# Rearranging the first two attentions of an attention and mixture-of-experts kernel

## The chip, the cores and the metric

The kernel runs on one core of one Trainium2 chip. The metric is the device time of one execution in microseconds (us). Before the change it is 366.93 us, the median of three runs (366.91 to 367.05). Engine names in the profile: PE is TensorE (matmuls; PEld its weight loads), DVE is VectorE, ACT is ScalarE, POOL is GpSimd, SP is SyncE. [...] everything that matmuls leave in PSUM is copied out by ScalarE or VectorE.

## The reference

Two stages follow each other. The first is grouped-query attention: 8 batches, 16 query heads, 4 key/value heads, 384 positions, head size 64, all float32. The second is a two-level gated mixture of experts over the 3072 tokens (8 x 384) with a model width of 1024: each token picks one of 4 groups by a softmax gate, then one of 4 experts in the group, and gets relu(x w1) w2 of that expert times both gate weights.

```python
scores = scale * np.matmul(q, k.transpose(0, 1, 3, 2))
attn = np.exp(scores - max); attn /= sum
out  = np.matmul(attn, v)                      # x: (3072, 1024)
...
g_idx = argmax(x @ w_group); e_idx = argmax(x @ w_expert[g_idx])
out[t] = g_w * e_w * (relu(x[t] @ w1[g, e]) @ w2[g, e])
```

## The kernel before

The program is written out by hand in order; each engine takes its instructions from a queue of its own, in the order in which the Python code emits them. Nothing is reordered later, so the place of a call in the code is its place in the queue of the engine that it uses.

**Attention.** For each batch there are 24 units: 4 groups of heads (g) times 6 chunks of 64 key positions (c). A unit u = 6g + c is: scores on PE (line 310, four matmuls into a PSUM tile of tag s, of which there are two), the exponential on ScalarE (line 316) into one of 13 buffers e, and the product with v on PE (line 329, eight matmul records, into a PSUM tile of tag o, one tile for each group, two in turn). `Attn.run` emits for each u: the scores of unit u + 2, the product of unit u, then `tail(u)`, and then the calls that a dictionary lists for u. The tail adds e tiles pairwise on GpSimd (line 336, at c = 1 and 3), reduces them on VectorE (line 343, four reductions for each group at c = 3, 4 and 5), and at the end of a group copies the PSUM result to xT, on VectorE (line 379) or on ScalarE (line 381).

**Normalising.** `collect` sums the reductions of some groups on VectorE (line 405), `sums` spreads them over partitions by matmuls (line 415) into a PSUM tile and takes the reciprocal on VectorE (line 419), `spread` transposes it into a tile rb (line 426), and `scale_x` multiplies xT by it (line 435). `cast` makes a bfloat16 copy xb. In `sums`, which "x" means the o tile that the current group does not use; the next group takes that tile over.

**Choosing an expert.** The kernel guesses for each batch one expert whose weights it fetches, from a mean of v: `sum_v` sums v over positions, on VectorE by one reduction (line 461) or on GpSimd by three adds (lines 467 to 469, the first of 768 elements a partition, the others of 256), `guess_mean` (474) and `guess_logits` (489) are small matmuls, `first_choice` (for batch 0) or `gate_softmax` (for the others, with the gate of the batch before it, lines 496 to 521) and `pick_index` (lines 576 to 586; line 580 is a comparison, 583 sums an index) run on VectorE. `pick` reads the index into a GpSimd register (line 590). `pick_w1` and `pick_w2` issue the fetches of 2 MB each (lines 560 and 566) from GpSimd's queue.

**Experts.** `moe_h` does two of the eight column blocks of w1: 16 matmuls (line 622) and a relu on ScalarE (line 626); `moe_y` does w2 (line 633) and scales the output (lines 658 and 660). `gate_logits` is the gate matmul (line 451).

**The first two batches.** Batch 0 has its scores, its products and its normalising in one run of 24 units. In batch 1 the reductions of the first groups are held back on a list (`hold`) and emitted at `a.release`. After unit 15 of batch 1 the run stops; the expert matmuls of batch 0 (`moe_h`, four times) stand in between, with the gate of batch 0 and the guess for batch 1; then units 16 to 23 follow, and `first_block` with `moe_y` of batch 0, the collect and the sums of the last two groups of batch 1, and the start of batch 2. Every later batch has a block of the same kind, which the change leaves as it is.

Of the kernel before, what the change touches and what calls it, by code (L numbers as in the profile page):

```python
# [9 lines left out]
F32 = mybir.dt.float32  # L10
BF16 = mybir.dt.bfloat16
# [7 lines left out]
def kernel(  # L19
# [11 lines left out]
    nc = tc.nc  # L31
    P = 128
    B, Hq, S, D = q.shape
    _, Hkv, _, _ = k.shape
# [5 lines left out]
    KQ = DM // P  # L40
    KG = KQ // Hkv
# [4 lines left out]
    NC = S // H2  # L46
# [14 lines left out]
    gpool = ctx.enter_context(tc.tile_pool(name="gate", bufs=1))  # L61
# [7 lines left out]
    def ps_tile(which, shape=None, dtype=F32):  # L69
        if which == "x":  # L70
            which = f"o{1 - turn['o']}"
        else:
            turn[which] = 1 - turn[which]
            which += str(turn[which])
        return psum.tile(shape or [P, 2, 512], dtype, name="ps_" + which)
# [4 lines left out]
    k16, qraw, vraw, qT, kT = {}, {}, {}, {}, {}  # L80
# [162 lines left out]
    def evac(eng, out_, in_):  # L243
        if eng is nc.scalar:
            eng.copy(out=out_, in_=in_)  # L245
        else:
            eng.tensor_copy(out=out_, in_=in_)
# [44 lines left out]
    xT, xb, reds = {}, {}, {}  # L292

    class Attn:
# [62 lines left out]
        def tail(self, u):  # L357
            b = self.b
            g, c = u // NC, u % NC
            z = u - c  # L360
            if c in (1, 3) and (b, u) != (1, 3):
                self.add(nc.gpsimd, u - 1)
            if (b, g) == (2, 0):
                for n in ((), (1,), (2, 0))[max(c, 3) - 3]:
                    self.reduce(g, n, (z, z + 4, z + 5)[n])
            elif c >= 3:
                self.reduce(g, c - 3, (z, z + 4, z + 5)[c - 3])
            if c == NC - 1:
                self.reduce(g, NR - 1, z + 2)
                if b not in xT:  # L370
                    if b == 1:
                        w = wpool.tile([P, KQ, F], BF16, name="w1")
                        xT[b] = w.rearrange("p a f -> p (a f)").bitcast(F32)[
                            :, :KQ * S].rearrange("p (a n) -> p a n", n=S)
                    else:
                        xT[b] = xpool.tile([P, KQ, S], F32, name="xT", bufs=1)
                dst, src = xT[b][:, KG * g:KG * (g + 1), :], self.oT[g][:, :, :S]
                if b > 1 and g < Hkv - 1 or (b, g) == (1, 1):
                    nc.vector.tensor_copy(out=dst, in_=src)  # L379
                else:  # L380
                    nc.scalar.copy(out=dst, in_=src)  # L381
# [40 lines left out]
    def spread(b, m, which=None):  # L422

        rb = gpool.tile([P, 2, S], F32, name="rb", bufs=2) if which is None else ps_tile(which)[:, :, :S]
        for r in range(2):
            nc.vector.transpose(  # L426
                out=rb[:, r].rearrange("p (j x) -> p j x", x=32),
                in_=inv[b][:, 2 * m + r].unsqueeze(2).to_broadcast([P, NB, 32]))
        return rb

    def scale_x(b, m, rb, eng):
        if b not in xb:
            xb[b] = xpool.tile([P, KQ, S], BF16, name="xb")
        x = xT[b][:, 2 * m:2 * m + 2, :]
        eng.tensor_mul(out=x, in0=x, in1=rb)  # L435

    def normalise(b, m, which=None):
        scale_x(b, m, spread(b, m, which), nc.vector)

    def cast(b, m, eng=None):  # L440
        ks = slice(2 * m, 2 * m + 2)
        evac(eng or nc.scalar, xb[b][:, ks, :], xT[b][:, ks, :])
# [3 lines left out]
    def gate_logits(b, pt):  # L446

        for kq in range(KQ):
            x = xT[b][:, kq, :].rearrange("p (c t i) -> p t c i", t=4, i=32)
            for t in range(4):  # L450
                nc.tensor.matmul(out=pt[32 * t:32 * t + 32, 0, :32 * SC], lhsT=wg[:, kq, :],  # L451
                                 rhs=x[:, t], start=(kq == 0), stop=(kq == KQ - 1))

    vsum = {}

    def sum_v(b, eng):

        vsum[b] = gpool.tile([P, Hkv, D], BF16, name="vsum")
        with nc.allow_low_precision("only serves a guess"):
            if eng is nc.vector:  # L460
                eng.tensor_reduce(out=vsum[b], in_=vraw[b].rearrange("p g (c d) -> p g d c", d=D),  # L461
                                  axis=AX.X, op=ALU.add)
                return
            n = NC // 2 * D
            t = gpool.tile([P, 2, S], F32, name="rb", bufs=2).rearrange(
                "p a s -> p (a s)").rearrange("p (g n) -> p g n", g=Hkv)
            eng.tensor_add(out=t, in0=vraw[b][:, :, :n], in1=vraw[b][:, :, n:])
            eng.tensor_add(out=t[:, :, :D], in0=t[:, :, :D], in1=t[:, :, D:2 * D])
            eng.tensor_add(out=vsum[b], in0=t[:, :, :D], in1=t[:, :, 2 * D:])

    def guess_mean(b, pt):

        for j in range(Hkv // 2):
            nc.tensor.matmul(out=pt[:, 1, j:j + 1],
                             lhsT=vsum[b][:, 2 * j:2 * j + 2, :].rearrange("p g d -> p (g d)"),
                             rhs=onesb[:, :1], start=True, stop=True)
# [6 lines left out]
    def guess_row(pt):  # L483
        return pt[:, 1, 64:64 + NW]

    def guess_logits(vm, pt):
        n = Hkv // 2
        for j in range(n):
            nc.tensor.matmul(out=guess_row(pt), lhsT=vm[:, j:j + 1].to_broadcast([P, P]),
                             rhs=wgd[:, j, :], start=(j == 0), stop=(j == n - 1))  # L490
# [78 lines left out]
    ers, w1s, w2s = {}, {}, {}  # L569
# [19 lines left out]
    def pick(b):  # L589
        ers[b] = nc.gpsimd.value_load(e_is[b][0:1, 0:1], min_val=0, max_val=NE - 1)  # L590
# [24 lines left out]
            j = 2 * c + h  # L615
            yield slice(h * H2, (h + 1) * H2), 2 * (j % SC) + j // SC

    def ffn_h(x, w1, hT, f0, which, mid=None):
        h = ps_tile(which)
        for jj in range(2):  # L620
            for kq in range(KQ):
                nc.tensor.matmul(out=h[:, jj, :S], lhsT=w1[:, kq, (f0 + jj) * P:(f0 + jj + 1) * P],  # L622
                                 rhs=x[:, kq, :], start=(kq == 0), stop=(kq == KQ - 1))
            if mid is not None and jj == 0:
                mid()
        nc.scalar.activation(hT[:, f0:f0 + 2, :], h[:, :, :S], ACT.Relu)  # L626

    def ffn_y(w2, hT, c, which, nhs=(0, 1), y=None, fs=None):
# [17 lines left out]

    hTs = {}

    def moe_h(b, f0, which, mid=None):
        if f0 == 0:  # L650
            hTs[b] = xpool.tile([P, FQ, S], BF16, name="hT", bufs=1)
        ffn_h(xb[b], w1s[b], hTs[b], f0, which, mid)

    def y_out(b, c, y, eng=None):
        ot = opool.tile([P, DM], F32, name="ot")
# [11 lines left out]
    def do(f, *a):  # L667
        return lambda: f(*a)
# [30 lines left out]
        pick_index(0)  # L699

    def first_fetch():
        pick(0)
        transposed(1)
        pick_w1(0)

# [20 lines left out]
    def second_scale():  # L726
# [3 lines left out]
    a = at[0]  # L730
    a.run(0, NU, {
        1: [do(first_q, GB, GB, "x", nc.vector)],
        3: [cast_k],
        4: [gate_matrix_b, do(sum_v, 0, nc.gpsimd)],
        6: [do(collect, 0, 0, 1)],
        7: [do(first_q, 2 * GB, 2 * GB, "x", nc.vector)],
        8: [do(first_k, 1, "x", nc.vector)],
        10: [do(sums, 0, 0, 1, "x"), do(normalise, 0, 0)],
        13: [first_guess],
        14: [do(cast, 0, 0)],  # L740
        15: [do(collect, 0, 1, 2), first_pick],
        19: [first_fetch, do(sums, 0, 1, 2, "x")],
        20: [first_spread],
        21: [first_scale],
# [4 lines left out]
    a = at[1]  # L749
    hold(a)  # L750
    a.run(0, FU, {
        4: [do(sums, 0, 2, Hkv, "x")],
        5: [second_scale, do(a.add, nc.gpsimd, 2), do(pick_w2, 0), do(sum_v, 1, nc.vector)],
        6: [do(normalise, 0, 3, "x")],
        9: [do(load_k, 2), do(load_q, 2), do(cast, 0, 2)],
        11: [a.release, do(collect, 1, 0, 2), do(cast, 0, 3)],
    })
    moe_h(0, 0, "s")
    load_v(2, nc.gpsimd)
    transposes(2)  # L760
    pt = ps_tile("x")
    gate_logits(0, pt)
    guess_mean(1, pt)
    vm = mean_copy(pt, nc.scalar)
    moe_h(0, 2, "s", do(sums, 1, 0, 2, pt))
    guess_logits(vm, pt)
    for m in range(2):
        normalise(1, m)
    moe_h(0, 4, "s")
    weights[0] = gate_softmax(0, pt, True)  # L770
    pick_index(1)
    moe_h(0, 6, "s")
    a.run(FU, NU, {21: [do(sum_v, 2, nc.gpsimd)]})

    def first_block():
# [111 lines left out]
    for c in range(SC):  # L887
# [5 lines left out]
        for i, (n0, n1) in enumerate(parts):  # L893
            y = ps_tile("so"[i % 2])
            for f in range(FQ):
                nc.tensor.matmul(out=y[:, 0, :n1 - n0], lhsT=hTs[B - 1][:, f, c * P:(c + 1) * P],  # L896
                                 rhs=w2s[B - 1][:, f, n0:n1], start=(f == 0), stop=(f == FQ - 1))
# [4 lines left out]
            for j, (ps, x) in enumerate(halves(c)):  # L902
                eng = nc.scalar if j and i % 2 == 0 else nc.sync
# [5 lines left out]
    with tc.For_i(0, n_left, 1):  # L909
# [19 lines left out]
        a = Attn(B)  # L929
# [4 lines left out]
        for m in range(Hkv):  # L934
            normalise(B, m)
            cast(B, m)
        x = xb[B]
        w1, w2 = fetch1(er), fetch2(er)
        m = gpool.tile([P, B, SC, NE], F32, name="pm")
        nc.vector.tensor_tensor(out=m, in0=cw_all,  # L940
                                in1=oh.unsqueeze(2).to_broadcast([P, B, SC, NE]), op=ALU.mult)
# [5 lines left out]
        hT = xpool.tile([P, FQ, S], BF16, name="hT", bufs=1)  # L947
# [43 lines left out]
```

The softmax here doesn't subtract the row's maximum and nothing guards it: scores larger than these inputs give would overflow.

## Time and profile before

| what | value |
|---|---|
| time, median of 3 | 366.93 us |
| span of the profiled execution | 366.1 us |
| busy: PE, DVE, ACT, POOL | 354.2, 275.7, 230.2, 160.5 us |
| mean of a reduction (343), of an add (336), of an exponential (316) | 946, 1836, 815 ns |
| mean of a copy of PSUM on DVE (379), on ACT (381) | 919, 799 ns |
| sum of v on DVE (461), mean | 2815 ns |

Busy time by stage, in us, from the table by stretches of the span:

| stretch, us | PE | DVE | ACT | POOL |
|---|---|---|---|---|
| 20 to 30 | 9.17 | 9.56 | 8.89 | 7.54 |
| 30 to 39 | 7.47 | 8.63 | 7.80 | 7.09 |
| 39 to 49.9 | 10.04 | 10.51 | 9.45 | 9.76 |
| 49.9 to 62.5 | 12.60 | 11.04 | 3.25 | 5.53 |
| 62.5 to 69.3 | 6.61 | 5.79 | 5.73 | 3.65 |
| 120 to 360 | 239.32 | 176.27 | 148.44 | 88.36 |

A line of a time line reads: start in us, duration in us, engine, line of the kernel, operation, output tile <- input tiles with sizes, number of instructions merged into the line, and in brackets how long the engine idled before it and what ended that. A line of the chain of waits reads: engine, tile and line that waited, what it waited for, us in total, times, longest. Ends of matmuls are modelled, and consecutive records overlap a little, so that durations are best read as distances from start to start.

### The profile page before, as it was taken

The numbers are of one execution on the slowest core, as the hardware profiler recorded it, in microseconds if no ns is written. First come the engines' busy times: TensorE is split into PE (matmuls) and PEld (weight loads), VectorE is DVE, ScalarE is ACT, GpSimd is POOL, SyncE is SP. The second block draws the span as 40 slices with busy tenths as digits, with TensorE's granted clock in tenths as the row PEclk, the third lists the DMA queues.
The fourth block names the chain that finished last, engine by engine and source line by source line (L and its number), as shares of the span: only waits on it lengthen the run. The fifth ranks groups of instructions, "written<-read, shape, count | busy, mean of one in ns | idle before, by whom it ended". The sixth has DMA issues, their size and how long they took to land.

```text
span 366.1 us, 9424 instructions
## 1 busy us (share of the span) xinstructions
PE 354.2 (97%) x3907; PEld 183.2 (50%) x3907; DVE 275.7 (75%) x506; ACT 230.2 (63%) x300; POOL 160.5 (44%) x127
## 2 busy tenths in 40 slices
PE   8999899999999999999999999999999999999992
PEld 4544455445455455554455445554545545555641
DVE  5689998858988498867989579884998659892230
ACT  5789853759926597267954599265972679544221
POOL 6886890736811476033730377113760258300000
PEclk9999999999999999999999999999999999999999
DMA  8973999999998999999999999989999899999333
GB/s 188 251 118 57 194 181 220 156 208 253 224 163 173 216 252 211 148 209 238 232 208 148 205 249 212 192 175 216 252 210 137 151 211 234 212 213 240 90 85 93
DMA packets 69902, 69.79 MB, mean 191 GB/s; under 512 B 35832, under 2 KB 49944, under 8 KB 69856
## 3 DMA queue, kind: packets, MB, share of 16 engines
q0 software_dynamic: 26864, 41.81, 65.1%
q1 hardware_dynamic: 42320, 26.40, 31.2%
q10 hardware_dynamic: 672, 0.93, 0.9%
q8 instruction: 32, 0.52, 0.5%
q14 instruction: 14, 0.11, 0.1%
HBM read 89.21 MB, written 12.58 MB: 278 GB/s over the span
## 4 chain that ended last, share of the span: by engine, by line
PE 87%; DVE 5%; ACT 2%; POOL 1%; issue 1%; DMA 1%; ACTq 0%
PE ps_o L329 28%; PE ps_s L622 22%; PE ps_s L633 13%; PE ps_s L310 8%; PE ps_o L633 7%; PE ps_o L451 3%; DVE red L343 3%; ACT e L316 2%; PE ps_s L896 2%; PE ps_o L622 1%; POOL e L336 1%; PE ps_o L896 1%; DMA w<-in_q_dram 1%; PE ps_o L415 1%; DVE rb L426 1%
## 5 line engine op out<-in xcount | busy, mean ns | idle before, releaser
L316 ACT ACTIVATE e<-ps_s 128x768 f32<-128x768 f32 x192 | 150.7, 815 | 20.1 <-PE ps_s L310 16.2
L329 PE MATMUL ps_o<-e,v_raw 64*64 64x384 f32 x1536 | 153.3, 483 | 1.4 <-DVE inv L419 1.4
L336 POOL TENSOR_TENSOR e<-e 128x768 f32<-128x768 f32 x64 | 116.4, 1836 | 62.6 <-ACT e L316 43.8
L343 DVE TRANSPOSE_TENSOR_REDUCE red<-e 128x24 f32<-128x768 f32 x128 | 114.1, 946 | 18.3 <-POOL e L336 18.3
L622 PE MATMUL ps_s<-xb,w 128*128 128x384 bf16 x480 | 81.0, 326 | 0.5 <-ACT e L316 0.5
L329 PEld LDWEIGHTS ps_o<-e,v_raw 64*64 64x64 f32 x1536 | 55.4, 133 | 39.7 <-issue 27.4
L622 PEld LDWEIGHTS <-w 128*128 128x128 bf16 x512 | 48.9, 98 | 36.2 <-issue 4.7
L310 PE MATMUL ps_s<-qT,kT 64*64 64x384 bf16 x768 | 63.7, 326 | 0.7 <-ACT e L316 0.2
L626 ACT ACTIVATE hT<-ps_s 128x768 bf16<-128x768 f32 x30 | 24.3, 811 | 61.0 <-PE ps_s L622 58.0
L633 PE MATMUL ps_s<-w,hT 128*128 128x512 bf16 x224 | 50.6, 379 | 0.0
L633 PEld LDWEIGHTS <-hT 128*128 128x128 bf16 x336 | 31.3, 97 | 36.6 <-issue 2.1
L310 PEld LDWEIGHTS <-kT 64*64 64x64 bf16 x768 | 24.2, 105 | 38.9 <-issue 37.1
L689 POOL COPY after<-qT 128x1 bf16<-128x1 bf16 x7 | 2.1, 304 | 79.5 <-DMA qT<-q_raw 78.1
L426 DVE STREAM_TRANSPOSE rb<-inv 128x384 f32<-128x384 f32 x62 | 32.0, 555 | 0.4
L658 ACT ACTIVATE ot<-ps_s,we 128x1024 f32<-128x1024 f32 x14 | 15.6, 1115 | 25.5 <-PE ps_s L633 12.1
L633 PE MATMUL ps_o<-w,hT 128*128 128x512 bf16 x112 | 26.5, 379 | 0.0
L435 DVE TENSOR_TENSOR xT<-xT,rb 128x768 f32<-128x768 f32 x25 | 24.0, 958 | 0.9
L245 ACT CAST xb<-xT 128x768 bf16<-128x768 f32 x27 | 21.7, 830 | 0.0
L461 DVE TENSOR_REDUCE vsum<-v_raw 128x256 bf16<-128x1536 f32 x6 | 16.9, 2815 | 0.0
L379 DVE COPY xT<-ps_o 128x768 f32<-128x768 f32 x18 | 16.5, 919 | 0.0
L660 DVE TENSOR_SCALAR ot<-ps_o,we 128x1024 f32<-128x1024 f32 x7 | 9.0, 1282 | 5.6 <-PE ps_o L633 4.6
L381 ACT COPY xT<-ps_o 128x768 f32<-128x768 f32 x10 | 8.0, 799 | 6.6 <-PE ps_o L329 6.6
(129 smaller groups left out, 201.4 us busy)
## 6 DMA issues: line engine op xcount, KB each, us to landing
w<-in_moe_w_dram POOLq DMA_DIRECT2D x16, 2048.0 KB, 23.4
out_dram<-ot SPq DMA_DIRECT2D x42, 256.0 KB, 6.6
q_raw<-in_q_dram POOLq DMA_DIRECT2D x7, 768.0 KB, 32.1
v_raw<-in_v_dram SPq DMA_DIRECT2D x12, 384.0 KB, 5.3
k<-in_k_dram POOLq DMA_DIRECT2D x7, 192.0 KB, 28.9
out_dram<-ot SPq DMA_DIRECT2D x7, 128.0 KB, 2.3
v_raw<-in_v_dram POOLq DMA_DIRECT2D x2, 384.0 KB, 11.5
w<-in_q_dram POOLq DMA_DIRECT2D x3, 192.0 KB, 7.5
```

The lines of the kernel that those rows point to most:

```text
L245: eng.copy(out=out_, in_=in_)
L310: nc.tensor.matmul(out=sT[r * H2:(r + 1) * H2, s, :S], lhsT=kT[b][s * D:(s + 1) * D, slot, ks], rhs=qT[b][s * D:(s + 1) * D, kq * SC:(kq + ...
L316: nc.scalar.activation(e.rearrange("p t (s x) -> p s t x", s=2), sT[:, :, :S].rearrange("p s (t x) -> p s t x", t=2), ACT.Exp, scale=scale)
L329: nc.tensor.matmul(out=oT[t * D:(t + 1) * D, r, :S], lhsT=vraw[b][r * H2:(r + 1) * H2, g, c * D:(c + 1) * D], rhs=self.e[u][r * H2:(r + 1) ...
L336: eng.tensor_add(out=self.e[u], in0=self.e[u], in1=self.e[u + 1])
L343: nc.vector.tensor_reduce(out=reds[self.b][:, g, n].rearrange("p t j -> p (t j)"), in_=self.e[u].rearrange("p t (j x) -> p (t j) x", x=32) ...
L426: nc.vector.transpose(out=rb[:, r].rearrange("p (j x) -> p j x", x=32), in_=inv[b][:, 2 * m + r].unsqueeze(2).to_broadcast([P, NB, 32]))
L435: eng.tensor_mul(out=x, in0=x, in1=rb)
L461: eng.tensor_reduce(out=vsum[b], in_=vraw[b].rearrange("p g (c d) -> p g d c", d=D), axis=AX.X, op=ALU.add)
L622: nc.tensor.matmul(out=h[:, jj, :S], lhsT=w1[:, kq, (f0 + jj) * P:(f0 + jj + 1) * P], rhs=x[:, kq, :], start=(kq == 0), stop=(kq == KQ - 1))
L626: nc.scalar.activation(hT[:, f0:f0 + 2, :], h[:, :, :S], ACT.Relu)
L633: nc.tensor.matmul(out=y[:, nh, :], lhsT=hT[:, f, c * P:(c + 1) * P], rhs=w2[:, f, nh * HALF:(nh + 1) * HALF], start=(f == 0), stop=(f == ...
```

## The change

It does five things, all in the first two batches:

- The sum of v of batch 0 is split: the large add stays near unit 5, the two small ones go to unit 11, behind the adds of e of units 7 and 9. The sum of v of batch 1 goes from VectorE (unit 5) to GpSimd (unit 15).
- The read of the expert index of batch 0 into the GpSimd register (`pick(0)`) goes from unit 19, behind the add of that unit, to unit 16, ahead of it.
- The copies of PSUM of (batch, group) (0, 3), (1, 0) and (1, 2) go from ScalarE to VectorE.
- In batch 1 the release of the held reductions goes from unit 11 to unit 8; the calls around it move by a unit, and the cast of the last quarter of batch 0 goes behind unit 15. The first `moe_h` takes the last two of eight steps of its contraction last, for both of its column blocks, so that it needs that cast late.
- The sums of the first two groups of batch 1 go from the second `moe_h` to the third, the guess for batch 1 from ahead of the second to behind the third, its logits into the fourth, with the gate and the index of batch 1 behind the fourth.

```diff
-                if b > 1 and g < Hkv - 1 or (b, g) == (1, 1):
+                if b > 0 and g < Hkv - 1 or (b, g) == (0, Hkv - 1):
                     nc.vector.tensor_copy(out=dst, in_=src)
...
+    def sum_v_halves(b, eng):
+        n = NC // 2 * D
+        t = gpool.tile([P, 2, S], F32, name="rb", bufs=2).rearrange(
+            "p a s -> p (a s)").rearrange("p (g n) -> p g n", g=Hkv)
+        eng.tensor_add(out=t, in0=vraw[b][:, :, :n], in1=vraw[b][:, :, n:])
+        vhalf[b] = t
+
+    def sum_v_rest(b, eng):
+        t = vhalf[b]
...
             eng.tensor_add(out=t[:, :, :D], in0=t[:, :, :D], in1=t[:, :, D:2 * D])
             eng.tensor_add(out=vsum[b], in0=t[:, :, :D], in1=t[:, :, 2 * D:])
...
+        last = KQ - KG if split else KQ
+        for k0, k1 in ((0, last), (last, KQ)):
+            for jj in range(2):
+                for kq in range(k0, k1):
...
     def first_fetch():
-        pick(0)
         transposed(1)
         pick_w1(0)
...
-        4: [gate_matrix_b, do(sum_v, 0, nc.gpsimd)],
+        4: [gate_matrix_b],
+        5: [do(sum_v_halves, 0, nc.gpsimd)],
...
+        11: [do(sum_v_rest, 0, nc.gpsimd)],
...
+        16: [do(pick, 0)],
         19: [first_fetch, do(sums, 0, 1, 2, "x")],
...
-        4: [do(sums, 0, 2, Hkv, "x")],
-        5: [second_scale, do(a.add, nc.gpsimd, 2), do(pick_w2, 0), do(sum_v, 1, nc.vector)],
+        4: [do(sums, 0, 2, Hkv, "x"), second_scale, do(a.add, nc.gpsimd, 2)],
+        5: [do(pick_w2, 0)],
         6: [do(normalise, 0, 3, "x")],
-        9: [do(load_k, 2), do(load_q, 2), do(cast, 0, 2)],
-        11: [a.release, do(collect, 1, 0, 2), do(cast, 0, 3)],
+        8: [a.release],
+        9: [do(load_k, 2), do(load_q, 2)],
+        10: [do(cast, 0, 2)],
+        11: [do(collect, 1, 0, 2)],
+        15: [do(sum_v, 1, nc.gpsimd)],
     })
-    moe_h(0, 0, "s")
+    cast(0, 3)
+    moe_h(0, 0, "s", split=True)
     load_v(2, nc.gpsimd)
     transposes(2)
     pt = ps_tile("x")
     gate_logits(0, pt)
+    moe_h(0, 2, "s")
+    moe_h(0, 4, "s", do(sums, 1, 0, 2, pt))
+    for m in range(2):
+        normalise(1, m)
     guess_mean(1, pt)
     vm = mean_copy(pt, nc.scalar)
-    moe_h(0, 2, "s", do(sums, 1, 0, 2, pt))
-    guess_logits(vm, pt)
-    for m in range(2):
-        normalise(1, m)
-    moe_h(0, 4, "s")
+    moe_h(0, 6, "s", do(guess_logits, vm, pt))
     weights[0] = gate_softmax(0, pt, True)
     pick_index(1)
-    moe_h(0, 6, "s")
     a.run(FU, NU, {21: [do(sum_v, 2, nc.gpsimd)]})
```

More of the change, by code (lines that the diff above doesn't have):

```diff
@@ L452, in gate_logits @@
                                  rhs=x[:, t], start=(kq == 0), stop=(kq == KQ - 1))
-    vsum = {}
+    vsum, vhalf = {}, {}
     def sum_v(b, eng):
@@ L463, in sum_v @@
                 return
[L464 to L467, printed above, removed]
+        sum_v_halves(b, eng)
+        sum_v_rest(b, eng)
+    def sum_v_halves(b, eng):
[6 more added lines that the diff above has]
+        t = vhalf[b]
+        if b not in vsum:
+            vsum[b] = gpool.tile([P, Hkv, D], BF16, name="vsum")
+        with nc.allow_low_precision("only serves a guess"):
             eng.tensor_add(out=t[:, :, :D], in0=t[:, :, :D], in1=t[:, :, D:2 * D])
@@ L616, in halves, with ffn_h @@
             yield slice(h * H2, (h + 1) * H2), 2 * (j % SC) + j // SC
-    def ffn_h(x, w1, hT, f0, which, mid=None):
+    def ffn_h(x, w1, hT, f0, which, mid=None, split=False):
         h = ps_tile(which)
[L620 to L625, printed above, removed]
+        last = KQ - KG if split else KQ
+        for k0, k1 in ((0, last), (last, KQ)):
+            for jj in range(2):
+                for kq in range(k0, k1):
+                    nc.tensor.matmul(out=h[:, jj, :S],
+                                     lhsT=w1[:, kq, (f0 + jj) * P:(f0 + jj + 1) * P],
+                                     rhs=x[:, kq, :], start=(kq == 0), stop=(kq == KQ - 1))
+                if mid is not None and jj == 0 and k0 == 0:
+                    mid()
         nc.scalar.activation(hT[:, f0:f0 + 2, :], h[:, :, :S], ACT.Relu)
@@ L647, with moe_h @@
     hTs = {}
-    def moe_h(b, f0, which, mid=None):
+    def moe_h(b, f0, which, mid=None, split=False):
         if f0 == 0:
             hTs[b] = xpool.tile([P, FQ, S], BF16, name="hT", bufs=1)
-        ffn_h(xb[b], w1s[b], hTs[b], f0, which, mid)
+        ffn_h(xb[b], w1s[b], hTs[b], f0, which, mid, split)
     def y_out(b, c, y, eng=None):
```

## The prediction, made before the result was known

> **What bounds the kernel now.** I read the busy shares first, then who waited for whom on TensorE, then TensorE record by record for its pauses, and last the time lines of the other engines around each pause.
>
> ```profile
> PE 354.2 (97%) x3907; PEld 183.2 (50%) x3907; DVE 275.7 (75%) x506; ACT 230.2 (63%) x300; POOL 160.5 (44%) x127
> ```
>
> PE is busy 97%. What a change of order can win is its pauses alone.
>
> ```profile
> PE ps_o L329 <- DVE inv L419: 1.4, 2, 0.8
> PE ps_o L415 <- DVE rsum L405: 0.9, 1, 0.9
> PE ps_s L622 <- ACT e L316: 0.5, 1, 0.5
> PE ps_s L310 <- ACT e L316: 0.2, 1, 0.2
> ```
>
> Record by record the pauses after 20 us are 0.83 (at 22.14), 0.61 (33.80), 0.92 (38.82), three of 0.11 (41.90, 45.43, 47.56), 0.53 (49.91) and 0.19 (66.29): 3.41 us, all in the two attentions that the change touches. From 66.3 to 360 us PE has no pause. The first three end on VectorE: its queue is the near-bound engine here (9.56 of 10 us busy from 20 to 30, 8.63 of 9 from 30 to 39, by the table by stage).
>
> The time lines of VectorE, GpSimd and PE show two things that the forecast hangs on.
>
> ```profile
> 28.92 1.62 DVE L580 TENSOR_SCALAR oh_all<-key,km 128x16 f32<-128x16 f32 x1
> 28.69 1.82 POOL L336 TENSOR_TENSOR e<-e 128x768 f32<-128x768 f32 x1 [1.06 <-ACT xT L381]
> 63.27 0.23 DVE L580 TENSOR_SCALAR oh_all<-key,km 128x16 f32<-128x16 f32 x1
> 65.46 1.82 POOL L336 TENSOR_TENSOR e<-e 128x768 f32<-128x768 f32 x1 [10.03 <-ACT e L316]
> ```
>
> The same 16-element instruction takes 1.62 us while a GpSimd add runs (28.69 + 1.82 = 30.51, where it ends) and 0.23 us with GpSimd idle. At 63.27 it is 2.2 us ahead of the next add.
>
> ```profile
> 70.91 0.48 DVE L405 TENSOR_REDUCE rsum<-red 128x48 f32<-128x192 f32 x1
> 72.88 0.42 PE L415 MATMUL ps_o<-rsum,half 128*64 128x24 f32 x8
> ```
>
> The last sums of batch 1 (line 415) need the collect of line 405, which ends at 71.39. PE gets there at 72.88: 1.49 us of slack. If PE gets there more than that earlier and VectorE doesn't, PE waits.
>
> [...] the 1.62 against 0.23 above; the other way round the add at 23.19 took 2.65 us instead of 1.82 beside the normalising multiply of 0.96. [...] the collect of 38.29 was held up only by four reductions ahead of it. [...]
>
> **The change part by part.** All durations are rows of before.
>
> (1) *sum of v, batch 0, split.* The same three adds (1.83 + 0.73 + 0.73), the two small ones later. The adds at 18.20 and 19.98 start 1.56 us earlier (16.64 instead of 18.20). The reduction at 20.06, which waited 1.32 us for them, can start behind the copy of kT, at 18.7: 1.36 us gained on VectorE. The reciprocal then ends at about 20.7 instead of 22.09, before PE wants its PSUM slot at 21.2. **The 0.83 pause goes**; ScalarE, continuously busy from 24.30, keeps about 0.75 of it.
>
> (2) *expert index read ahead of an add.* The add of 28.69 now waits behind the index. GpSimd idles from about 26.3 until the index is there, so line 580 takes 0.23, not 1.62. With the 1.36 of (1): index at 28.2 instead of 30.94, the add at 29.0 (index read 0.86, as 30.94 to 31.80), reciprocal at 30.7 instead of 33.47, PE wants it at 32.3. **The 0.61 pause goes.** The w1 fetch is issued at 31.5 instead of 32.54 and lands in 14.1 us at 45.6, before its use at about 46.7.
>
> (3) *copies of PSUM on VectorE.* Three copies of 0.95 (0.87 from start to start) leave ScalarE (0.8 each), one in batch 0 and two in batch 1. That of batch 0 stands ahead of the third collect: VectorE reaches it at 36.3 instead of 38.29, ending at 36.8. PE, 1.5 us early, wants it at 36.3: **0.5 of the 0.92 stays**. PE is now 2.0 us early.
>
> (4) *batch 1 up to the experts.* VectorE loses the sum of v (2.88) and gains a copy; the eight held reductions start at 41.7 instead of 46.5, but stand now ahead of the copy of (1,1): four from 41.7, four to 48.6, copy to 49.6. ScalarE loses a copy and a cast, so two of the three 0.11 pauses and the 0.53 go (the stall of 0.82 before the e at 49.04, on a buffer held by an add, goes too). Expert matmuls start at 46.7 (49.91 before), their first 2.65 us end at 49.4; the gate matmuls of line 451 take the PSUM slot that the copy empties and start at 49.6, 52.59 before: 3.0 us early. The split of the contraction costs nothing: 12 matmuls (2.0 us) run ahead of the late cast (0.8).
>
> (5) *sums of batch 1 one expert step later.* They move behind line 622's second step. Gate 1.46, one step 2.65 and half a step with 0.06 of setup 1.4 after 49.6: **A = 55.1**, where before they were at 55.51. So 2.6 of the 3.0 us are not handed on to VectorE, which idles from 51.3 to A.
>
> (6) *behind A.* In before, VectorE started the reciprocal at A + 0.54, line 580 at A + 7.76, t (line 583) at A + 8.03, reductions at A + 8.32. Its work is the same. On PE one step of 2.65 us less lies between A and the second part of attention: its first scores start at A + 7.01 - 2.65 + 0.07 = A + 4.43, and the add of unit 18 (2.94 behind them before: 65.46 - 62.52) at **A + 7.37**, 0.39 us ahead of line 580. [...] line 580 waits until the add ends, A + 9.19. The next add is ready by then: its pv ends 4.38 behind the first scores (67.30 - 62.52 less the 0.19 pause with its refill, 0.4), and 0.17 to start gives A + 8.98. [...] t [...] waits for its end, A + 11.0. Reductions start at A + 11.15, 2.83 later than undisturbed. Queued behind on VectorE: three reductions (2.61), the new copy (0.87), four reductions (3.56), collect (0.48), 0.06 to PE: 7.58. PE gets the sums at 55.1 + 11.15 + 7.58 = 73.85, against 72.88. It would be there at A + 4.43 + 6.42 (the second part, 62.52 to 69.33 less a pause) + 3.56 (line 633) = A + 14.4, so **it waits some 4.3 us, and ends 1.0 us later than before.** Afterwards PE has no pause, so 366.93 + 1.0 = **367.9**.
>
> (7) *nothing more.* The sum of v of batch 1 on GpSimd (3.4 us) ends at about 55.5, used at A + 1.7 = 56.8; GpSimd was idle there for 10 us. The fetches of batch 2 move up by about 1 us, and the later w1 lands 7 us ahead of use (94.0 against 101.65), so no transfer sets the end.
>
> **Unknown costs.** [...] none costs 0; one 1.23 (9.19 + 0.02 less 7.99); two 2.83; a third (the comparison key, 0.4 earlier, or the cast of the index against the sum of v at 66) about 1.7 more. I take two, since both margins (0.39 and 0.2 us) point that way. A itself: 54.4 (nothing but PE) to 55.7 (GpSimd, back to back from 29 us, slips by 0.6).
>
> **The rivals.** *One meeting only* (the second add is 0.3 us later than worked out): 55.1 + 9.55 + 7.58 = 72.2, 0.65 early: 366.3. For it: the margin is 0.2 us. Against it: the adds follow each other with no gap wherever both inputs are ready. *No meeting* (PE held up before unit 18, or the chain quicker): 55.1 + 8.32 + 7.58 = 71.0, 1.85 early: 365.1; against it, 0.39 and 0.66 us (line 580 and t) on the same side. *Three meetings*: 1.7 later than the forecast, 369.6; for it, the sum of v of batch 2 stands next in GpSimd's queue. *All pauses closed*, VectorE keeping up: 366.93 - 3.4 = 363.5; against it, the copy and the later A both lie on VectorE.
>
> **How the numbers follow.** Two meetings 0.38, one 0.20, none 0.15, three 0.17, all pauses closed 0.04, the rest (another new wait, a slip of A) 0.06. Low end 365.4: cuts off half of "none" and all of "closed"; high end 369.6. Faster by over 0.2% (under 366.2): none, closed and 0.4 of one: 0.27. Slower by over 0.2% (over 367.66): 0.65 of two, three, and most of the rest: 0.48. The rest, 0.25, is within.
>
> **What would show it.** Right in the first part: no wait of line 329 for the reciprocal, line 580 at about 27.5 taking 0.23, a wait of line 415 of 0.5 near 37. Right in the second: line 580 near 63 lasting 1.3 or more and t behind it the length of an add, the four last reductions of batch 1 ending past 73, and one wait of line 415 for the collect of 3 us or more near 70 to 74 (more with two meetings, less with none). Wrong if line 580 near 63 shows 0.23, if line 415 comes before 72.5, or if PE waits for w1 or for the sum of v near 57.

## The result, and the profile after

The changed kernel takes **370.59 us** (median of four runs, 370.22 to 371.14) against 366.92 (366.82 to 367.05) before: 3.7 us slower, ratio 1.0101, 95% interval 1.0083 to 1.0118. The forecast was 367.9 us, with a range up to 369.6: the right direction and, as it turns out, the right chain of waits up to the last sums of batch 1, but less than a third of the loss.

Line numbers shift in the new file: the comparison of line 580 is now 591, t (583) is 594, the index read (590) is 601, matmuls of w1 (622) are 635 and of w2 (633) are 647. First the busy shares and who waited for whom on PE, after the change (us in total, times, longest):

```profile
PE 354.4 (96%) x3907; PEld 184.0 (50%) x3907; DVE 275.7 (75%) x508; ACT 228.3 (62%) x297; POOL 163.0 (44%) x130
```

```profile
PE ps_o L415 <- DVE rsum L405: 4.8, 2, 4.2
...
PE ps_o L451 <- DVE w L379: 0.4, 1, 0.4
```

The waits of line 329 for the reciprocal and those for ScalarE are gone, as forecast. What stands in their place is one wait of 4.2 us at the last sums of batch 1, a rest of 0.6 at the third sums, and 0.4 at the gate matmuls for the copy of group (1, 1). PE is busy for the same 354 us as before.

The time line of VectorE and of GpSimd where the 4.2 us come from:

```profile
62.67 1.55 DVE L591 TENSOR_SCALAR oh_all<-key,km 128x16 f32<-128x16 f32 x1
64.25 1.74 DVE L594 SCALAR_TENSOR_TENSOR t<-eidx,oh_all 128x16 f32<-128x16 f32 x1
...
66.10 2.69 DVE L343 TRANSPOSE_TENSOR_REDUCE red<-e 128x24 f32<-128x768 f32 x3
68.71 0.92 DVE L379 COPY w<-ps_o 128x768 f32<-128x768 f32 x1
69.56 3.54 DVE L343 TRANSPOSE_TENSOR_REDUCE red<-e 128x24 f32<-128x768 f32 x4
73.13 0.48 DVE L405 TENSOR_REDUCE rsum<-red 128x48 f32<-128x192 f32 x1
```

```profile
62.37 3.58 POOL L336 TENSOR_TENSOR e<-e 128x768 f32<-128x768 f32 x2 [5.80 <-ACT e L316]
```

Two 16-element instructions last 1.55 and 1.74 us instead of 0.23 and 0.17. The two adds of GpSimd run from 62.37 to 65.95; the first instruction ends with the first add (64.22 and 64.18 us), the second with the second (65.99 and 65.95). Each of the two is a meeting, as the prediction calls it. Behind them on VectorE stand three reductions, the new copy, four reductions and the collect, and the collect is what PE waits for. In the other seven batches of this profile no add runs beside lines 591 and 594, and they take 0.23 and 0.17 us. In the first attention the same comparison, which had taken 1.62 us, is free:

```profile
27.38 0.23 DVE L591 TENSOR_SCALAR oh_all<-key,km 128x16 f32<-128x16 f32 x1
```

Now PE, in its own time line and in the table by stretches (columns: stretch, its length, busy us of PE with the number of instructions, PEld, DVE, ACT, POOL, then the granted TensorE clock, share of DMA, GB/s):

```profile
65.85 3.63 PE L647 MATMUL ps_s<-w,hT 128*128 128x512 bf16 x16
73.66 0.63 PE L415 MATMUL ps_o<-rsum,half 128*64 128x24 f32 x8 [4.19 <-DVE rsum L405]
74.22 4.87 PE L647 MATMUL ps_s<-w,hT 128*128 128x512 bf16 x16
78.93 1.89 PE L647 MATMUL ps_o<-w,hT 128*128 128x512 bf16 x8
```

```profile
66.00:69.60 3.60, 3.47 (x16) 1.36 (x14) 3.57 (x6) 2.35 (x4) 3.19 (x3) 1.00 0.87 167
69.60:73.70 4.10, 0.04 (x2) 0.04 (x2) 4.05 (x7) 0.00 (x0) 1.26 (x3) 0.96 0.97 203
73.70:77.00 3.30, 3.30 (x16) 1.48 (x17) 3.07 (x9) 1.11 (x1) 2.33 (x3) 0.53 1.11 206
77.00:82.30 5.30, 5.30 (x85) 2.96 (x84) 2.16 (x4) 2.57 (x3) 0.00 (x0) 1.00 1.08 207
```

The same 16 matmuls of line 647 take 3.63 us ahead of the pause and 4.87 behind it. The third column from the right shows why: the granted clock is 0.53 from 73.7 to 77. In the records the half clock lasts 3.413 us, and while it lasts the matmuls start every 0.427 us instead of every 0.216. That is what the forecast lacked. From before to after, the last sums start 0.78 us later (72.88, 73.66), and the gate matmuls of batch 1, behind the 24 matmuls of line 647, 2.23 us later (78.52, 80.75), by their rows before and after:

```profile
78.52 1.53 PE L451 MATMUL ps_o<-w,wg 128*32 128x96 f32 x64
80.75 1.53 PE L451 MATMUL ps_o<-w,wg 128*32 128x96 f32 x64
```

So 0.78 us is the wait and 1.45 us the clock. From there to the last matmul both kernels take the same 280.80 us.

The head and the tail of the execution differ a little from run to run. The mean granted clocks of the four runs, 0.985 to 0.994, don't tell how often the clock dropped among the matmuls, since they take in the tail. In this profile the last matmul ends at 361.55 us, and from 366.90 us the clock is at half again, at no cost to PE; in a second profile of the changed kernel (the last run of the next section) this begins at 364.59 us already, and the mean is 0.990 instead of 0.994. From 6.2 us to the last matmul both profiles have one stretch at half clock, the one behind the pause.

### The profile page after: what moved, and what is told of

The parts are those of the page before. It is cut to its first block, busy times and chain, and to the rows that moved or that the text cites. A ratio compares the mean times of both kernels' runs of the same rounds, so it can differ in the third digit from the quotient of the medians.

```text
span 368.1 us, 9424 instructions
## 1 busy us (share of the span) xinstructions
PE 354.4 (96%) x3907; PEld 184.0 (50%) x3907; DVE 275.7 (75%) x508; ACT 228.3 (62%) x297; POOL 163.0 (44%) x130
## 4 chain that ended last, share of the span: by engine, by line
PE 83%; DVE 11%; POOL 1%; issue 1%; DMA 1%; ACT 0%; ACTq 0%; POOLq 0%
PE ps_o L329 26%; PE ps_s L635 21%; PE ps_s L647 13%; PE ps_s L310 7%; PE ps_o L647 7%; DVE red L343 6%; PE ps_o L451 3%; PE ps_s L915 2%; PE ps_o L635 1%; PE ps_o L915 1%; DMA w<-in_q_dram 1%; POOL e L336 1%; PE ps_o L415 1%; DVE rb L426 1%; DVE w L379 1%
## 5 line engine op out<-in xcount | busy, mean ns | idle before, releaser
L647 PE MATMUL ps_s<-w,hT 128*128 128x512 bf16 x224 | 51.9, 386 | 0.0
L379 DVE COPY xT<-ps_o 128x768 f32<-128x768 f32 x19 | 17.5, 919 | 0.0
L461 DVE TENSOR_REDUCE vsum<-v_raw 128x256 bf16<-128x1536 f32 x5 | 14.0, 2801 | 0.0
L571 POOL DMA_DIRECT2D w<-in_moe_w_dram x8 | 7.3, 916 | 14.3 <-PE ps_s L310 11.9
```

Of the source, the lines that this page charges most:

```text
L647: nc.tensor.matmul(out=y[:, nh, :], lhsT=hT[:, f, c * P:(c + 1) * P], rhs=w2[:, f, nh * HALF:(nh + 1) * HALF], start=(f == 0), stop=(f == ...
```

## The experiments

All are compared with runs of the kernel before on the same chip (medians 366.98, 366.90 and 366.78 us in the three groups). Where the text gives the time of an instruction, it is from the profile of that kernel.

### The index of batch 1 read ahead of the add

```diff
-    a.run(FU, NU, {21: [do(sum_v, 2, nc.gpsimd)]})
+    a.run(FU, NU, {17: [do(pick, 1)], 21: [do(sum_v, 2, nc.gpsimd)]})
...
-        if b != 2:
+        if b > 2:
             pick(b)
```

> The changed kernel, with the index of batch 1 read into the GpSimd register ahead of the add of unit 18 instead of behind the second part of attention. Theory [...]: with GpSimd waiting, line 591 near 62.7 takes 0.23 us instead of 1.55 and t (line 594) 0.17 instead of 1.74; the seven reductions and the copy behind them come 2.9 us earlier, so PE gets the last sums at about 70.8 instead of 73.66, waits about 1.5 us instead of 4.2, and the TensorE clock doesn't drop: about 364.9 us (2 under before). Rival A ([...] VectorE is late because of the copies that it was given): line 415 comes at most 1 us earlier, 369.5 or more. Rival B (GpSimd's wait for the index is itself costly, since its adds come later): the reductions of units 18 and 20 wait for their adds and line 415 stays later than 72.5.

Measured: 365.70 us, ratio 0.9969 (0.9955 to 0.9983): 4.9 us under the changed kernel. This profile begins late (PE waits 1.48 us for gate weights ahead of 8.70 us, and a stretch of half clock follows at 9.33 to 12.74), so that all of it stands 2.95 us later than in the changed kernel; distances are what counts.

VectorE and GpSimd:

```profile
65.62 0.23 DVE L591 TENSOR_SCALAR oh_all<-key,km 128x16 f32<-128x16 f32 x1
65.88 0.18 DVE L594 SCALAR_TENSOR_TENSOR t<-eidx,oh_all 128x16 f32<-128x16 f32 x1
```

```profile
67.07 3.60 POOL L336 TENSOR_TENSOR e<-e 128x768 f32<-128x768 f32 x2 [7.55 <-ACT e L316]
```

and PE:

```profile
73.73 0.42 PE L415 MATMUL ps_o<-rsum,half 128*64 128x24 f32 x8 [1.30 <-DVE rsum L405]
74.08 3.63 PE L647 MATMUL ps_s<-w,hT 128*128 128x512 bf16 x16
```

The adds start 0.8 us behind the index, the two instructions are short, the last sums come at 73.73 - 2.95 = 70.78 (expected 70.8), PE's wait shrinks to 1.30 us, and the 16 matmuls behind it take the full-clock 3.63. Both rivals fall: the two meetings cost VectorE 2.9 us (1.55 + 1.74 in the changed kernel, less 0.23 + 0.18 here), and GpSimd's wait costs nothing, since VectorE waits for none of the later adds. The time is 0.8 us over the expected 364.9; the next run misses by as much.

### The pause filled with matmuls

```diff
-        sums(1, 2, Hkv, "o")
+        po = ps_tile("o")
+        for _ in range(17):
+            nc.tensor.matmul(out=po[:, 0, :], lhsT=onesb[:, :P], rhs=onesb, start=True, stop=True)
+        sums(1, 2, Hkv, po)
```

> The changed kernel, with 17 matmuls of ones (512 columns, 0.216 us each, results unused) put in PE's queue ahead of the last sums of batch 1, into the free half of the same PSUM tile: they fill the pause of 4.2 us with work and alter nothing else. Theory (the pause lets the TensorE clock drop to half for 3.4 us or more, and that costs more than the late sums): line 415 still near 73.7, no stretch at half clock before the end, matmuls of line 647 behind it at 0.216 us from start to start instead of 0.427; about 367.7 us (0.8 over before). Rival (the clock is a side effect of the late sums and costs nothing): 370.6 as the changed kernel.

Measured: 368.55 us, ratio 1.0041 (1.0028 to 1.0054), and 368.41 to 368.70 in five runs, where the changed kernel spreads over 0.9 us and more. The last sums stay where they were, and the matmuls behind them are fast:

```profile
69.72 3.83 PE L805 MATMUL ps_o<-onesb 128*128 128x512 bf16 x17 [0.23 <-DVE w L379]
73.69 0.42 PE L415 MATMUL ps_o<-rsum,half 128*64 128x24 f32 x8
74.04 3.63 PE L647 MATMUL ps_s<-w,hT 128*128 128x512 bf16 x16
```

So the clock alone is worth 370.59 - 368.55 = 2.0 us of the median; the changed kernel again, at the end of the study, gives 1.8. Between the two profiles it is 1.42 us at the start of the last matmuls (360.51 and 359.09), close to the 1.45 above; where the rest of the 2.0 lies, the runs don't show. The theory's 367.7 is missed by 0.8: 1.57 us over before instead of 0.8. A likely reason lies in the kernel before; its second profile, below, has it.

### Half the filling

The same with 8 matmuls, so that PE pauses for 2.09 us.

> The changed kernel with 8 filling matmuls instead of 17 ahead of the last sums of batch 1, so that PE pauses for about 2.2 us instead of 4.2. If only long pauses let the clock drop: no stretch at half clock, line 647 behind it at 0.216 us, 368.5 us as with the full fill. If any pause does: a stretch at half clock follows and the time lies near the 370.6 of the changed kernel.

Measured: 370.08 us, ratio 1.0074 (1.0052 to 1.0097), in nine runs from 367.61 to 371.06. In the profile the pause of 2.09 us is followed by a stretch of half clock and the 16 matmuls take 5.16 us:

```profile
73.65 0.52 PE L415 MATMUL ps_o<-rsum,half 128*64 128x24 f32 x8 [2.09 <-DVE rsum L405]
74.10 5.16 PE L647 MATMUL ps_s<-w,hT 128*128 128x512 bf16 x16
```

In three runs out of nine the mean clock is 0.994 to 0.996 and the time 367.6 to 368.8, in six 0.989 or 0.990 and 369.8 to 371.1. So, by times and mean clocks, the clock dropped behind this pause in six of the nine runs; one of the six, at 369.80 us, is the profiled one, and for the others it is my estimate. Behind the pauses of 1.30 us (with the index read ahead) and 1.36 us (the run below on the copies) the profiles show no drop: the 16 matmuls take 3.63 us in both.

The clock records of the 13 profiles of this study show what goes with the drop besides the length. Between two changes of the clock within a profile lies always a whole multiple of 3.413 us (in the changed kernel 68.267 us, 20 times as much, ahead of the drop, 3.413 in it and 290.133, 85 times, behind it), and the series begins at another moment in each execution: behind the same pause, half clock begins at 73.36 us in the first profile of the changed kernel and at 74.45 us in the second. Cut each profile into such stretches of 3.413 us and add up in each the time without a matmul. From 12 us on, every stretch at full clock with 2.09 us or more of it was followed by half clock (16 cases, 13 of them at the end, where the matmuls stop), and none with 1.95 us or less was. The pause of 2.09 us lies whole in one stretch here (70.41 to 73.82 us); a border inside it would have split it between two. That the three faster runs had such a border is a guess of mine and not shown, since they have no profile. The start of the kernel is apart: with the index read ahead, a stretch with 1.48 us without a matmul (5.91 to 9.33 us) was followed by half clock.

### The sums of batch 1 where they were

```diff
-    moe_h(0, 2, "s")
-    moe_h(0, 4, "s", do(sums, 1, 0, 2, pt))
+    moe_h(0, 2, "s", do(sums, 1, 0, 2, pt))
+    moe_h(0, 4, "s")
```

> The changed kernel, with the sums of the first two groups of batch 1 back in the second expert step, as before the change; all else as changed. Theory (the sums one step later are what brings line 591 and t together with the adds): the reciprocal starts at about 52.8 instead of 55.43, the chain of the gate then waits for its logits at 58.0 and ends at about 61.7, before the add of unit 18 at 62.4; line 591 takes 0.23, the reductions start at 61.6, the collect ends at about 69.1, PE has no wait at line 415 and no drop of clock: about 363.6 us. Rival (VectorE is too late in any case, by the copies): a wait of 1 us or more remains at line 415 and the time is 365 or more.

Measured: 364.67 us, ratio 0.9942 (0.9924 to 0.9960): one line of the change moved back makes it 2.3 us faster than before instead of 3.7 slower. VectorE, PE and GpSimd:

```profile
61.30 0.23 DVE L591 TENSOR_SCALAR oh_all<-key,km 128x16 f32<-128x16 f32 x1
...
68.89 0.49 DVE L405 TENSOR_REDUCE rsum<-red 128x48 f32<-128x192 f32 x1
```

```profile
69.56 0.42 PE L415 MATMUL ps_o<-rsum,half 128*64 128x24 f32 x8
```

```profile
62.53 3.60 POOL L336 TENSOR_TENSOR e<-e 128x768 f32<-128x768 f32 x2 [5.17 <-ACT e L316]
```

The comparison ends 1.0 us ahead of the add, and PE gets the sums when it comes for them, 4.1 us earlier than in the changed kernel. The rival, that VectorE would be late in any case, falls. The time is 1.1 us over the expected 363.6, though the mechanism is as stated.

### The copies back on ScalarE

```diff
-                if b > 0 and g < Hkv - 1 or (b, g) == (0, Hkv - 1):
+                if b > 1 and g < Hkv - 1 or (b, g) == (1, 1):
```

> The changed kernel, with the three copies of PSUM back on ScalarE. Theory (the copies are a minor term: 0.87 us each on VectorE): line 415 near 37 has no wait, [...] PE gets the last sums at about 72.5, after a wait of some 3.5 us: 366.5 us if the clock holds, 368 to 370 if it drops. Rival (the copies on VectorE are the cause of the loss): 365 us or less, with no wait over 1 us at line 415.

Measured: 365.47 us, ratio 0.9964 (0.9951 to 0.9977). Here my theory is wrong by 1.0 to 4.5 us and the rival's number is nearly met, though not for its reason alone: PE still waits, 1.36 us. PE, VectorE and GpSimd show what I had not seen:

```profile
70.52 0.42 PE L415 MATMUL ps_o<-rsum,half 128*64 128x24 f32 x8 [1.36 <-DVE rsum L405]
```

```profile
61.96 1.55 DVE L591 TENSOR_SCALAR oh_all<-key,km 128x16 f32<-128x16 f32 x1
63.54 0.17 DVE L594 SCALAR_TENSOR_TENSOR t<-eidx,oh_all 128x16 f32<-128x16 f32 x1
```

```profile
61.66 1.81 POOL L336 TENSOR_TENSOR e<-e 128x768 f32<-128x768 f32 x1 [5.80 <-ACT e L316]
63.68 1.83 POOL L336 TENSOR_TENSOR e<-e 128x768 f32<-128x768 f32 x1 [0.20 <-PE ps_s L310]
```

There is one meeting instead of the two that my theory counted on. With the copy of group (1, 2) on ScalarE, PE is held up by 0.195 us near 62, the second add starts 0.20 us behind the first instead of at once, and t slips in between. The last sums come 3.14 us earlier than in the changed kernel: 0.70 because the sums of the first groups come earlier (54.26 against 54.97; 0.29 of it is a head that is shorter in this profile), 1.57 for the second meeting, 0.87 for the copy. Behind the remaining wait of 1.36 us the clock does not drop in this profile (the 16 matmuls take 3.63 us), so what the drop cost is saved as well. The 0.2 us of margin that the prediction gave for the second meeting was real: it holds with the copies moved, and not without.

### The first attention's edits alone

The kernel before, with only the sum of v of batch 0 split and its index read ahead of the add.

```diff
-        4: [gate_matrix_b, do(sum_v, 0, nc.gpsimd)],
+        4: [gate_matrix_b],
+        5: [do(sum_v_halves, 0, nc.gpsimd)],
...
+        11: [do(sum_v_rest, 0, nc.gpsimd)],
...
+        16: [do(pick, 0)],
```

> The kernel before, with the two edits of the first attention alone: the sum of v of batch 0 split, and its expert index read ahead of an add. Theory (these two take 2.8 us out of VectorE's chain up to the third collect): all three waits near 22, 34 and 38 go, PE gets the third sums at about 36.0 instead of 38.82; in batch 1 nothing is rearranged, so line 580 near 60 is about 1.5 us ahead of the next add, takes 0.23, and the slack at the last sums stays as before: 2.5 to 2.8 us under before, about 364.3 us. Rival (what is gained in the first attention is lost in batch 1, as in the changed kernel): a wait over 1 us at the last sums, 366 us or more.

Measured: 365.29 us, ratio 0.9955 (0.9938 to 0.9972), 1.6 us under before, where 2.5 to 2.8 were expected. The mechanism is as stated: none of the three waits of PE near 22, 34 and 38 is left, and nothing is lost in batch 1. The size is not. The kernel before, run once more, gives a likely reason.

### The kernel before, once more

> The kernel before, unchanged, for a second profile: its timed runs have spans of 364.6 to 365.7 us, the profile shown has 366.1. If the difference is in the first attention (the comparison of line 580 beside the add meets it in one run and misses it in another), line 580 near 28 shows another duration than 1.62; if it is at the head or the tail, lines 329 and 415 have the same distances as before.

Measured: one run, with a span of 366.0 us. The comparison near 28 takes 1.81 us here, so it meets the add again; that guess is wrong. What differs is in front of it. GpSimd's time line, first as shown in the profile that the prediction used, then in the second one:

```profile
14.35 0.51 POOL L288 CAST w<-w 128x384 bf16<-128x384 f32 x1 [1.07 <-DMA w<-in_k_dram]
14.81 1.83 POOL L467 TENSOR_TENSOR rb<-v_raw 128x768 f32<-128x768 f32 x1
```

```profile
13.64 0.51 POOL L288 CAST w<-w 128x384 bf16<-128x384 f32 x1
14.11 1.83 POOL L467 TENSOR_TENSOR rb<-v_raw 128x768 f32<-128x768 f32 x1
```

In the first, half of k of batch 0 landed late and GpSimd stood 1.07 us for it, so that everything behind it on GpSimd came late too; in the second it did not wait, PE has no pause at 22 us, and from the first sums of line 415 to the second it takes 8.52 us instead of 9.45. With the first part of the change alone it takes 8.52 as well. So **splitting the sum of v brings nothing when k lands in time**. When k is late it does what it was meant to: in the profile with the copies back on ScalarE, GpSimd stands 1.16 us for the same half of k, PE has no pause near 22 us, and the two sums are 8.52 us apart all the same. Waits of GpSimd for k of over 1 us are in 2 of the 13 profiles. By this account the 1.6 us come from the index (no run has that edit alone), which together with what follows takes the distance from the second sums to the third from 9.56 us (both profiles of before) to 7.98. The second profile has a late head of its own (0.65 us for gate weights), so its span is no shorter. In the repeats the spans of before are mostly 364.6 to 365.7 us: the profile that I predicted from, at 366.1, was 0.4 to 1.5 us slower than these, and its first pause is a likely part of that, shown in one profile out of two.

### What the good parts make together

With the sums early, the copies on VectorE one by one. First, that of group 3 of batch 0 back on ScalarE:

```diff
-                if b > 0 and g < Hkv - 1 or (b, g) == (0, Hkv - 1):
+                if b > 0 and g < Hkv - 1:
```

> The changed kernel with the sums of batch 1 back in the second expert step (as in the run before this one) and with the copy of group 3 of batch 0 back on ScalarE. Theory (that copy, 0.87 us ahead of the third collect, makes the wait of 0.59 us at line 415 near 37): the wait goes, PE is 0.5 us earlier from there on, the copies of batch 1 keep their place; 0.3 to 0.6 us under the kernel with early sums alone, about 364.2 us. Rival (ScalarE, which takes the copy, then holds PE up by as much): the same 364.7 us, with a wait of line 310 or 329 near 33.

Measured: 363.89 us, ratio 0.9916 (0.9898 to 0.9935). The wait at line 415 is gone, the 0.5 us at line 451 is left. Then also that of group 0 of batch 1:

```diff
-                if b > 0 and g < Hkv - 1 or (b, g) == (0, Hkv - 1):
+                if b > 1 and g < Hkv - 1 or (b, g) in ((1, 1), (1, 2)):
```

> The changed kernel with the sums of batch 1 in the second expert step and, of the three copies, only that of group 2 of batch 1 on VectorE. Theory (the wait of 0.49 us at line 451 near 49 is for the copy of group 1 of batch 1, which stands behind that of group 0 on VectorE): the wait goes, since VectorE has 0.87 us less ahead of it; ScalarE, with one copy more, holds PE up by 0.1 to 0.3 instead; 0.2 to 0.4 us under the kernel with two copies moved, 363.6 us. Rival (ScalarE is the bound near 40): 364 us or more.

Measured: **363.53 us**, ratio 0.9904 (0.9871 to 0.9937): the lowest median of the study, 3.3 us under the kernel before and 7 under the changed one. And with none moved:

> The changed kernel with the sums of batch 1 in the second expert step and none of the three copies moved: what the copies on VectorE bring once the sums are early. Theory: VectorE has 0.87 us less ahead of the last sums, which PE doesn't wait for in either case; ScalarE's copy of group 2 of batch 1 brings back the pause of 0.2 us (0.4 with its refill) near 62: 363.9 us, 0.3 over the run with that one copy moved. Rival (each copy on VectorE costs PE time): less than with it.

Measured: 364.11 us, ratio 0.9923 (0.9894 to 0.9951). In the two profiles the last sums come at 68.99 with the copy of (1, 2) on VectorE and 69.36 without: 0.37 us for the pause of 0.2 and what PE loses behind it, as expected (0.4). The intervals of these three overlap. Counted from the first sums of line 415 in each profile, the last sums come after 49.37 us with two copies moved, 49.30 with one and 49.67 with none. So one copy is ahead of none by the pause, but an order between one and two is not shown: the wait of 0.49 us at line 451 is gone, as expected, and PE gains only 0.07 us by it.

### The changed kernel again

> The changed kernel, unchanged, on the chip of these runs: the pause of 4.2 us at line 415 near 70 in every profile, the half clock behind it; runs differ by the number of stretches of 3.4 us at half clock, 369.5 to 371.5 us, mean granted clock 0.985 to 0.994.

Measured: 370.37 us, ratio 1.0098 (1.0064 to 1.0133), 370.20 to 371.62 in six runs, mean clock 0.986 to 0.991; the pause is 4.20 us at 73.81, with half clock behind it, as in the first runs. That runs differ by the number of stretches at half clock is not shown: this profile, too, has one among the matmuls.

## Why the prediction was wrong in size, point by point

- *What bounds the kernel, and that only pauses count*: right. PE's work is the same, and the time moves with its pauses and, as the prediction had not thought of, with its clock.
- *(1), "the 0.83 pause goes; ScalarE keeps about 0.75 of it"*: the mis-sized term on the side of gains. The pause was made by a late landing of k in the one profile that I had, which another profile of the same kernel doesn't show. The wait came from a landing, not from the order of the instructions alone: GpSimd's cast stood 1.07 us for k in one profile of this kernel and not in the other. The row was in the profile, and I did not ask how often it happens. About 0.8 us too much gain.
- *(2), the index ahead of the add*: right. Comparison 0.23 at 27.38 (forecast 27.5), index at 28.02 (28.2), no pause at 34. Together with the split it brings 1.6 us.
- *(3), the copy ahead of the third collect*: right. A pause of 0.6 at 36.6 (forecast 0.5 near 37).
- *(4) and (5), experts at 46.7, gate at 49.6, sums at A = 55.1*: measured 46.32, 49.51 and 54.97. The gate does wait for the copy of (1, 1), 0.41 us. All right.
- *(6), two meetings*: right, 1.55 and 1.74 us. That the comparison lasts until an add ends was measured in the profile of before (1.62 us at 28.92); that t does too was my estimate, since t took 0.17 or 0.18 us in all eight batches there, and the changed kernel bears it out. Of what follows from them, the reductions start at A + 11.13 (forecast 11.15), the last sums at 73.66 (73.85), after 4.2 us of waiting (4.3). The third meeting did not happen: the cast of the index takes its usual 0.15 at 66.03, while an add of GpSimd's sum of v of batch 2 runs (65.92 to 67.74).
- *"Afterwards PE has no pause, so 366.93 + 1.0 = 367.9"*: **this step failed**. It takes PE behind the pause to be as fast as before. Behind the pause of 4.2 us the TensorE clock is at half for a stretch of 3.413 us: 1.45 us in the profiled run, 1.8 to 2.0 of the median. With the pause filled with matmuls the clock stays up (16 matmuls in 3.63 us instead of 4.87) and the time is 368.55 us. The profile of before does not show such a cost: from 20 us to the end of its last matmul, at 359.32 us, its longest pause is 0.92 us and its clock is full throughout.
- *The sum*: 1.0 forecast, less 0.2 (the sums came that much earlier), plus 0.8 for (1) and 2.0 for the clock make 3.6; measured are 3.7. The 0.8 is an estimate, the pause of 0.83 us that the runs without a late k don't have; of the 2.0, the profile locates 1.45.
- *(7), nothing more*: right. The profile shows no wait for the sum of v at the guess or for w1.
- *The rivals*: one meeting, no meeting and all pauses closed were given for the changed kernel, and none came. But experiments show each of them: one meeting with the copies back, none with the index read ahead or the sums early, and no pause of PE over 0.14 us after 17 us with the sums early and one copy moved. That this last one took 363.53 us, with 363.5 given for it, is in part luck, since 0.83 of the 3.4 us that were to be gained came from the late k.

## What to carry to other kernels

A short instruction of VectorE that stands in a chain someone waits for should not run beside a row of GpSimd adds, if a profile shows it to last until an add ends, as the comparison and t do here (1.55 and 1.74 us instead of 0.23 and 0.17): let GpSimd wait for its result first, or move the chain to a time when GpSimd idles. When work of one engine is moved later by a step, count where its followers now meet the other engines, not only whether someone waits for it at once: here 2.65 us of delay cost 6 us. And a pause of TensorE has to be priced at its length plus what the clock may lose behind it: here a pause of 4.2 us cost 1.45 us more in the profile, behind one of 2.09 us the clock dropped too, and behind those of 1.30 and 1.36 us it did not. A pause that can't be taken away can be filled with matmuls that nobody uses (368.55 us here instead of 370.59).

## What the runs showed of the hardware that was not expected

- *Half clock behind a pause of PE*: in the profile of the changed kernel and in that of its repeat, a stretch of 3.413 us at clock 0.5 follows the pause of 4.2 us, and matmuls of 512 columns start every 0.427 us instead of 0.216. What goes with the drop in these 13 profiles is the time without a matmul within one stretch of a series of 3.413 us that begins at another moment in each execution: behind 2.09 us or more the clock dropped, behind 1.95 us or less it did not, but for one case at the start (1.48 us).
- *Two instructions in a row each lasted until an add ended*: in the changed kernel, with adds back to back on GpSimd, the comparison ends at 64.22 us, when the first add does (64.18), and t, which starts 0.03 us later, lasts 1.74 us, until the second add ends at 65.95. With the copies back on ScalarE the second add starts 0.20 us behind the first, and t takes 0.17 us.
- *The cast of one element to an index was not held up*: in the changed kernel it takes 0.15 us at 66.03, beside an add of GpSimd that runs from 65.92 to 67.74.
